# Expert tiles placed between the transforms of later batches, with the mixed rows scattered to their places by expert

## The chip, the cores and the metric

One core of a Trainium2 chip runs the kernel. The metric is device time in microseconds of one execution, median of several runs. The profiled execution is one run of its own, with its own time.

## What is computed

```python
X = np.fft.rfft(x, axis=1)                       # x: (8, 2496, 256)
y = np.fft.irfft(X * (filt_r + 1j * filt_i), n=2496, axis=1)
x = y.reshape(19968, 256)
expert_idx = token_ids * np.int64(2654435761) % np.int64(8)
for e in range(8):                               # w1: (8, 256, 1024), w2: (8, 1024, 256)
    mask = expert_idx == e
    out[mask] = np.maximum(x[mask] @ w1[e], 0.0) @ w2[e]
```

A filter in the frequency domain mixes the 2496 positions of each of 8 batches, channel by channel. Then each of the 19968 rows goes through the expert (two matrices with a ReLU between) that its token id names. All of it is in float32.

## The kernel before

**Transforms.** A batch's transform of length 2496 = 39 x 64 is done in three parts, each a row of matmuls, with a copy through DRAM between them. Part 1 (`stage1`, L161) has 8 units per batch: a load of `x`, two matmuls `pa` with the table `wf_t`, copies to `t1`, a store to the DRAM tile `d1`. Part 2 (`stage2`, L209) has 10 steps: `forward` makes `pb` from `d1` (tile `t2`, loaded four frequencies at a time by `load2`), VectorE multiplies it by the two filter tables, and one step later `back` makes `pc` with the table `e_t`; the result goes to the DRAM tile `d2`. Part 3 (`stage3`, L219) has 8 units: a load of `d2` (tile `t4`), two matmuls `pd` with `wi_t`, copies to `o`, and a store of 78 partitions to `xtok` in DRAM, where the rows stand in token order. Part 2 needs a whole `d1`, part 3 a whole `d2`. The loop at L372 runs part 2 of batch b, part 1 of b+1 and part 3 of b-1 beside each other, by a fraction of the step that each piece gets.

**Routing.** `route()` (L274) works out on VectorE from the token ids how many rows each expert has, and for each row a slot: rows of one expert lie together, padded to full tiles of 128. `slot_token` (156 indirect transfers on POOL) writes each row's number to its slot, and `idx_all` reads the list back. `chunk_i` holds for each of the NCH = 163 tiles its expert, and whether that differs from the expert two tiles before.

**Experts.** After the last transform the PSUM and SBUF pools are closed and opened anew. Per tile: `gather` (L425) fetches 128 rows of `xtok` by an indirect transfer, `turn` (L434) transposes them on TensorE, `up` (L442) does 16 matmuls with w1 into two PSUM tiles that ACT and VectorE clip at zero into `ht`, `down` (L458) does 8 matmuls with w2, VectorE copies the result, and POOL scatters it to `out`. Weights have two buffers that the tiles use in turn; `load_weights` (L343) loads a pair of 1 MB each on SP's queue, on the condition that the expert is another.

**Order.** All plain loads and stores are issued on SP's queue (constants on ACT's). In the transform stage a scheduler orders the engines' instructions; for the tiles SP's order is the program's.

## Time and profile before

| | |
|---|---|
| median of 3 runs | 1828.25 us (1825.52 to 1828.43) |
| the profiled execution | 1827.75 us |
| its span, first to last instruction | 1826.1 us |
| mean granted TensorE clock | 0.958 |
| TensorE busy | 1679.4 us (92%) |
| VectorE, ACT, POOL busy | 416.9, 248.8, 486.8 us |
| transfers | 208.91 MB, mean 114 GB/s |

The span is what the trace covers; the time has 1.65 us more around it. Busy time of TensorE is a union of overlapping matmuls whose ends are modelled, so a busy stretch is not one at its peak. PEclk is the granted clock as a part of the full one.

### The profile page before, as it was taken

How to read it: one execution, taken by the hardware profiler on the slowest of the kernel's cores; microseconds unless marked ns; L12 is line 12 of the kernel's file. 1: busy time of each engine (PE TensorE's matmuls, PEld its weight loads, DVE VectorE, ACT ScalarE, POOL GpSimd, SP SyncE). 2: the span in 40 equal slices, each digit the busy share in tenths (PEclk: the TensorE clock that was granted, in tenths of full speed). 3: DMA queues.
4: the chain of work that ended last, by engine and by line, in shares of the span. 5: the costliest groups of instructions: out<-in, count | busy, mean ns of one | idle time of the engine just before them, and what ended most of it. 6: DMA issues, size and time to landing. Idle time of an engine off the chain costs nothing.

```text
span 1826.1 us, 26491 instructions
## 1 busy us (share of the span) xinstructions
PE 1679.4 (92%) x9626; PEld 1393.6 (76%) x9626; DVE 416.9 (23%) x766; ACT 248.8 (14%) x416; POOL 486.8 (27%) x493
## 2 busy tenths in 40 slices
PE   4598579789798699999999999999999999999998
PEld 1365245445455299999999999999999999999997
DVE  2432123233232012112111211211211221121121
ACT  1122122222232100000000000000000000000000
POOL 0477760000000122222222222222222222222221
PEclk9999788898899599999999999999999999999999
DMA  9788887787786411131131131131131131122110
GB/s 214 187 226 238 212 245 218 207 254 223 206 257 180 137 36 35 57 111 36 38 126 39 38 126 38 36 129 39 35 130 36 39 129 36 39 83 81 39 36 8
DMA packets 111533, 208.91 MB, mean 114 GB/s; under 512 B 17546, under 2 KB 76556, under 8 KB 111085
## 3 DMA queue, kind: packets, MB, share of 16 engines
q1 hardware_dynamic: 88683, 158.47, 30.5%
q0 software_dynamic: 20640, 41.93, 7.4%
q10 hardware_dynamic: 2082, 6.82, 1.6%
q8 instruction: 78, 1.28, 0.3%
q14 instruction: 50, 0.41, 0.1%
HBM read 432.44 MB, written 83.92 MB: 283 GB/s over the span
## 4 chain that ended last, share of the span: by engine, by line
issue 47%; PE 24%; POOL 18%; DMA 8%; SPq 2%; POOLq 1%; DVE 1%; ACT 0%; ACTq 0%; DVEq 0%
POOL xg L429 9%; POOL out_dram L466 9%; PE pa L166 7%; PE pc L199 7%; PE pd L224 6%; DMA x<-in_x_dram 4%; PE pb L183 4%; DMA t<-d 3%; SPq L175 1%; SPq L206 0%; POOLq L466 0%; POOLq L429 0%; DMA d<-t 0%; ACT g L202 0%; DMA d<-g 0%
## 5 line engine op out<-in xcount | busy, mean ns | idle before, releaser
L450 PEld LDWEIGHTS ups<-xt,w 128*128 128x128 f32 x5216 | 610.0, 192 | 8.4
L450 PE MATMUL ups<-xt,w 128*128 128x128 f32 x5216 | 610.6, 275 | 0.0
L462 PE MATMUL dps<-w,ht 128*128 128x256 f32 x2608 | 589.9, 379 | 0.0
L462 PEld LDWEIGHTS dps<-w,ht 128*128 128x128 f32 x2608 | 482.8, 190 | 58.9
L429 POOL DMA_INDIRECT xg<-xtok,idx_all x163 | 167.1, 1025 | 733.3 <-DMA xtok<-o 366.5
L466 POOL DMA_INDIRECT out_dram<-osb,idx_all x163 | 166.2, 1019 | 488.9 <-DVE osb L465 488.9
L454 ACT ACTIVATE ht<-ups 128x512 f32<-128x512 f32 x163 | 97.3, 597 | 1089.1 <-PE ups L450 1089.1
L456 DVE TENSOR_SCALAR ht<-ups 128x512 f32<-128x512 f32 x163 | 112.7, 692 | 524.2 <-PE ups L450 524.2
L166 PE MATMUL pa<-x,wf_t 78*80 78x512 f32 x256 | 151.8, 731 | 82.4 <-DMA x<-in_x_dram 75.4
L335 POOL DMA_INDIRECT slot_tokens<-token,key_i x156 | 151.9, 973 | 110.7 <-DVE key_i L319 63.5
L465 DVE COPY osb<-dps 128x256 f32<-128x256 f32 x163 | 69.2, 425 | 423.2 <-PE dps L462 423.2
L166 PEld LDWEIGHTS pa<-x,wf_t 78*80 78x80 f32 x256 | 44.4, 179 | 157.7 <-issue 108.4
L224 PE MATMUL pd<-t,wi_t 80*78 80x512 f32 x256 | 135.6, 667 | 25.6 <-DMA t<-d 25.6
L199 PE MATMUL pc<-p,e_t 128*128 128x256 f32 x640 | 156.2, 388 | 0.0
L199 PEld LDWEIGHTS pc<-p,e_t 128*128 128x128 f32 x640 | 125.8, 197 | 22.5 <-issue 3.6
L188 DVE TENSOR_TENSOR p<-pb,filt 128x512 f32<-128x512 f32 x160 | 103.0, 686 | 147.9 <-PE pb L183 146.9
L183 PEld LDWEIGHTS pb<-t,d_t 128*128 128x128 f32 x320 | 65.5, 206 | 70.1 <-issue 53.8
L224 PEld LDWEIGHTS pd<-t,wi_t 80*78 80x78 f32 x256 | 41.1, 164 | 96.2 <-issue 81.2
L183 PE MATMUL pb<-t,d_t 128*128 128x256 f32 x320 | 90.4, 409 | 23.5 <-DMA t<-d 22.9
L202 ACT COPY g<-pc 128x512 f32<-128x512 f32 x80 | 46.9, 586 | 189.9 <-PE pc L199 181.9
L137 ACT COPY t<-pa 80x512 f32<-80x512 f32 x86 | 49.5, 582 | 152.9 <-PE pa L166 140.2
L437 PE MATMUL xps<-ident,xg 128*128 128x128 f32 x326 | 62.8, 275 | 7.9 <-DMA xg<-xtok,idx_all 7.9
(54 smaller groups left out, 247.5 us busy)
## 6 DMA issues: line engine op xcount, KB each, us to landing
w<-in_moe_w_dram SPq DMA_DIRECT2D x326, 1024.0 KB
d<-t SPq DMA_DIRECT2D x64, 320.0 KB
t<-d SPq DMA_DIRECT2D x80, 256.0 KB
d<-g SPq DMA_DIRECT2D x80, 256.0 KB
t<-d SPq DMA_DIRECT2D x64, 320.0 KB
x<-in_x_dram SPq DMA_DIRECT2D x64, 312.0 KB
xtok<-o SPq DMA_DIRECT2D x64, 312.0 KB
xg<-xtok,idx_all POOLq DMA_INDIRECT x163, 2.8
```

Source lines behind the costliest of these rows:

```text
L166: nc.tensor.matmul(out=ps[0:NK], lhsT=wf_t[:], rhs=xt[:, 2 * i:2 * i + 2, :], start=True, stop=True)
L183: nc.tensor.matmul(out=ps[:, i, :], lhsT=d_t[:, s, :], rhs=self.t2[s // SG][:, s % SG, :], start=True, stop=True)
L188: nc.vector.tensor_tensor(out=pt[:], in0=ps[:], in1=f_t[k][:, 2 * u:2 * u + 2, :], op=OP.mult)
L199: nc.tensor.matmul(out=ps[:, i, :], lhsT=e_t[:, k, 2 * u + i, :], rhs=pr[k][:, i, :], start=(k == 0), stop=(k == 1))
L224: nc.tensor.matmul(out=ps[0:NR], lhsT=wi_t[:], rhs=t4[:, 2 * i:2 * i + 2, :], start=True, stop=True)
L335: st = nc.gpsimd.indirect_dma_start(out=slot_dram[:, None], out_offset=bass.IndirectOffsetOnAxis(ap=key_i[:, j:j + 1], axis=0), in_=token[ ...
L429: nc.gpsimd.indirect_dma_start(out=xg[c][:, t, :], out_offset=None, in_=xtok[:], in_offset=bass.IndirectOffsetOnAxis(ap=idx_all[:, j:j + 1 ...
L450: nc.tensor.matmul(out=ps[:, i, :], lhsT=w1[:, dp, fp * P:(fp + 1) * P], rhs=xt[c][:, dp, :], start=(dp == 0), stop=(dp == DP - 1))
L454: nc.scalar.activation(out=dst, in_=ps[:], func=AF.Relu)
L456: nc.vector.tensor_scalar_max(dst, ps[:], 0.0)
L462: nc.tensor.matmul(out=ps[:], lhsT=ht[:, fp, :], rhs=w2[:, fp, :], start=(fp == 0), stop=(fp == FP - 1))
L466: st = nc.gpsimd.indirect_dma_start(out=out[:], out_offset=bass.IndirectOffsetOnAxis(ap=idx_all[:, c:c + 1], axis=0), in_=o[:], in_offset= ...
```

## The change

The rows' places are now made in stages. `stage_tiles` and the new part of `route` count, for the first 2, 4, 6 and all 8 batches, how many full tiles of 128 rows each expert has by then; the tiles that become full in a stage lie together in the DRAM tensor `xs`, by expert. So the first 30 tiles hold rows of batches 0 and 1 alone, the tiles up to 70 rows of the first 4 batches, those up to 108 of the first 6. Part 3 no longer stores to `xtok`: each unit makes 4 indirect scatters on POOL that put 78 rows each at their places in `xs`. A row is 272 words: 256 of data, and 16 that hold its number, which the scatter to `out` takes as its index. Places that stay empty in the last stage get 7 scatters of blank rows. A tile is then a plain load of 128 rows on SP's queue; the gathers and the `slot_token` transfers go.

The order is written out by hand for all engines. The list `pre` runs the parts 1 of batches 0 to 2, the parts 2 and 3 of batches 0 and 1, the routing, and the first two weight pairs. The list `main` gives every other transform piece a place among the tiles: a piece with key k runs in tile floor(k), between that tile's `turn` of the next tile and its `down`. Three batch steps lie in tiles 0 to 24, two more up to 62, the rest up to 100. Within a stage the tiles alternate between its lower and upper half. The two weight loads of a pair are issued apart, after `up` and after `down`. PSUM is shared: 4 buffers for the transforms, 2 for `up`, 1 each for `turn` and `down`. Copies of part 1 are all on ACT, those of part 3 all on VectorE; stores to `d1` and `d2` are issued on ACT's queue.

```diff
+STAGES = (2, 4, 6, 8)
+G = len(STAGES)
...
+def stage_tiles():
+    ends = [(S * b - E * (TB - 1)) // TB // 2 * 2 for b in STAGES[:-1]] + [NT]
+    out, first = [], 0
+    for end in ends:
+        half = (end - first + 1) // 2
+        out.append([first + i // 2 + (half if i % 2 else 0) for i in range(end - first)])
+        first = end
+    return out
...
+    xs = nc.dram_tensor("xs", (NT * TB, W), F32)
+    slot_dram = nc.dram_tensor("slots", (N,), I32)
...
+    ctx.enter_context(tc.manual_schedule())
...
+    fps = pool(ctx, "fps", 4, PSUM)
+    xps = pool(ctx, "xps", 1, PSUM)
+    ups = pool(ctx, "ups", 2, PSUM)
+    dps = pool(ctx, "dps", 1, PSUM)
...
-            nc.sync.dma_start(out=self.d1_rows[:, XG * u:XG * u + XG, :], in_=t1[:])
+                nc.scalar.copy(out=t1[:, 2 * i:2 * i + 2, :], in_=ps[0:NK])
+            nc.scalar.dma_start(out=self.d1_rows[:, XG * u:XG * u + XG, :], in_=t1[:])
...
-                    nc.sync.dma_start(out=self.d2[a0:a0 + SG, :, :].rearrange("s n c -> n s c"),
-                                      in_=self.g[64 * p:64 * p + 64, :, :])
+                    nc.scalar.dma_start(out=self.d2[a0:a0 + SG, :, :].rearrange("s n c -> n s c"),
+                                        in_=self.g[64 * p:64 * p + 64, :, :])
...
-            o = opool.tile([NR, XG, C], F32, name=f"o_{self.b}_{u}", tag="o")
+            o = opool.tile([NR, XG, W], F32, name=f"o_{self.b}_{u}", tag="o")
+            nc.gpsimd.iota(o[:, :, C:].bitcast(I32), pattern=[[1, XG], [0, W - C]],
+                           base=self.b * S + XG * u, channel_multiplier=N2 // 2)
             for i in range(XG // 2):
                 ps = fps.tile([P, 2, C], F32, name=f"pd_{self.b}_{u}_{i}", tag="f")
                 nc.tensor.matmul(out=ps[0:NR], lhsT=wi_t[:], rhs=t4[:, 2 * i:2 * i + 2, :],
                                  start=True, stop=True)
-                evac(o[:, 2 * i:2 * i + 2, :], ps[0:NR])
-            st = nc.sync.dma_start(out=self.rows(xtok.ap(), u), in_=o[:])
-            tc.declare_no_dep(st.ins, group="xtok_rows", reason="distinct rows")
-            tc.add_to_no_dep_group("xtok_rows", st.ins)
-    batches = [Batch(0)]
-    for u in range(2):
+                nc.vector.tensor_copy(out=o[:, 2 * i:2 * i + 2, 0:C], in_=ps[0:NR])
+            for i in range(XG):
+                j = XG * u + i
+                scatter(o[:, i, :], sidx[:, self.b, j:j + 1], f"xs_{self.b}")
+    def scatter(rows, index, group):
+        st = nc.gpsimd.indirect_dma_start(
+            out=xs[:], out_offset=bass.IndirectOffsetOnAxis(ap=index, axis=0),
+            in_=rows, in_offset=None, bounds_check=NT * TB - 1, oob_is_err=False)
+        for other in ["xs_pad", "xs_read"] + [f"xs_{b}" for b in range(B)]:
+            tc.declare_no_dep(st.ins, group=other, reason="distinct rows")
+        tc.add_to_no_dep_group(group, st.ins)
...
+    def weights(i, which):
+        if i >= NT:
+            return
+        if i < 2:
+            if which == 0:
+                ws[i] = [wpool.tile([P, DP, F], F32, name=f"w1_{i}"), wpool.tile([P, FP, C], F32, name=f"w2_{i}")]
+        elif which == 0:
+            ws[i] = ws[i - 2]
+        e = nc.sync.value_load(chunk_i[0:1, 0, i:i + 1], min_val=0, max_val=E - 1)
+        kw = {}
+        if i >= 2:
+            kw = {"cond": nc.sync.value_load(chunk_i[0:1, 1, i:i + 1], min_val=0, max_val=1)}
+        if which == 0:
+            nc.sync.dma_start(out=ws[i][0][:], in_=moe_w1[bass.ds(e, 1)].rearrange("one (dp p) f -> p (one dp) f", p=P), **kw)
+        else:
+            nc.sync.dma_start(out=ws[i][1][:], in_=moe_w2[bass.ds(e, 1)].rearrange("one (fp p) d -> p (one fp) d", p=P), **kw)
...
+        nc.vector.tensor_tensor(acc[:], run[:], over(off[:, 0, :], NJ), op=OP.add)
+        for g in range(1, G):
+            nc.vector.tensor_tensor(tmp[:], run[:], over(full_t[:, g, :], NJ), op=OP.is_ge)
+            nc.vector.tensor_tensor(tmp[:], tmp[:], over(step[:, g, :], NJ), op=OP.mult)
+            nc.vector.tensor_tensor(acc[:], acc[:], tmp[:], op=OP.add)
+        nc.vector.tensor_mul(acc[:], acc[:], mask[:])
...
+        nc.gpsimd.dma_start(out=slot_dram[:].rearrange("(p j) -> p j", p=P), in_=slot_i[:])
+        nc.gpsimd.dma_start(out=sidx[:], in_=slot_dram[:].rearrange("(b p n) -> p b n", b=B, p=NR))
...
+        for q in range(NQP):
+            scatter(blank[:], at_i[:, q:q + 1], "xs_pad")
...
+        ps = fps.tile([P, 2, C], F32, name="ce_ps", tag="f")
+        for q in range(2):
+            nc.tensor.matmul(out=ps[0:1, 0, q * P:(q + 1) * P], lhsT=seg[:, q:q + 1], rhs=ident[:],
+                             start=True, stop=True)
...
+    def part1(b, t0, t1):
+        bt = batches[b]
+        at = [t0 + (t1 - t0) * u / NU for u in range(NU)]
+        step = (t1 - t0) / NU
+        out_ = [(at[u], lambda u=u: bt.stage1(u)) for u in range(NU)]
+        out_ += [(at[u] - 1.9 * step, lambda u=u: bt.load1(u)) for u in range(3 if b == 0 else 0, NU)]
+        return out_
...
+        out_ += [(max(at[2 * g] - 4.5 * step, ready), lambda g=g: bt.load2(g)) for g in range(NS // SG)]
...
+    pre = part1(0, -100, -81) + [(-80.9, route), (-80.8, dup_filters)]
+    pre += part1(1, -79, -60) + part2(0, -75, -50, -80)
+    pre += part2(1, -45, -25, -59) + part3(0, -44, -25)
+    pre += part3(1, -20, -1) + part1(2, -19, -2)
+    pre += [(-30 + i, lambda i=i: (weights(i, 0), weights(i, 1))) for i in range(2)]
+    pre.sort(key=lambda t: t[0])
+    bounds = [0.0, 9.0, 18.0, 25.0, 44.0, 63.0, 84.0, 101.0]
+    main, ready = [], 0.0
+    for k, b in enumerate(range(3, B + 2)):
+        t0, t1 = bounds[k], bounds[k + 1]
+        d = t1 - t0
+        if b - 1 < B:
+            main += part2(b - 1, t0 + 0.01 * d, t0 + 0.9 * d, ready)
+        if b < B:
+            main += part1(b, t0 + 0.02 * d, t0 + 0.62 * d)
+            ready = t0 + 0.65 * d
+        if b - 2 >= 2:
+            main += part3(b - 2, t0 + 0.3 * d, t1)
+    main.sort(key=lambda t: t[0])
+    for _, piece in pre:
+        piece()
+    rctx.close()
...
+    def load(i):
+        q = tiles[i]
+        xg[i] = gath.tile([P, W], F32, name=f"xg_{i}", tag="xg")
+        ld = nc.sync.dma_start(out=xg[i][:], in_=xs[q * TB:(q + 1) * TB, :])
+        for b in range(STAGES[stage_of[i]], B):
+            tc.declare_no_dep(ld.ins, group=f"xs_{b}", reason="the tiles of a stage hold tokens of its batches alone")
+        tc.add_to_no_dep_group("xs_read", ld.ins)
...
-            out=out[:], out_offset=bass.IndirectOffsetOnAxis(ap=idx_all[:, c:c + 1], axis=0),
+            out=out[:], out_offset=bass.IndirectOffsetOnAxis(ap=xg[i][:, C:C + 1].bitcast(I32), axis=0),
...
-    ctx.enter_context(tc.manual_schedule(engines={mybir.EngineType.SP}))
-    for c in range(min(3, NCH)):
-        gather(c)
+        del xg[i]
+    for i in range(4):
+        load(i)
     turn(0)
-    for c in range(NCH):
-        ht = work.tile([P, FP, CH], F32, name=f"ht_{c}", tag="ht")
-        if c + 3 < NCH:
-            gather(c + 3)
-        up(c, ht)
-        if c + 1 < NCH:
-            turn(c + 1)
-        down(c, ht)
-        if c + 2 < NCH:
-            load_weights(c + 2)
+    for i in range(NT):
+        ht = work.tile([P, FP, TB], F32, name=f"ht_{i}", tag="ht")
+        if i + 4 < NT:
+            load(i + 4)
+        up(i, ht)
+        weights(i + 2, 0)
+        if i + 1 < NT:
+            turn(i + 1)
+        while main and main[0][0] < i + 1:
+            main.pop(0)[1]()
+        down(i, ht)
+        weights(i + 2, 1)
+    assert not main
```

TensorE at an expert tile before (`ups` are the up matmuls, `xps` the transposes of the next tile, `dps` the down matmuls):

```order
L450 MATMUL ups_0_9642<-xt_9601,w_1_1001 128x128 x8
L450 MATMUL ups_1_9652<-xt_9601,w_1_1001 128x128 x8
L437 MATMUL xps_9662<-ident,xg_9510 128x128 x2
L462 MATMUL dps_9667<-w_1_1002,ht_9637 128x256 x8
L450 MATMUL ups_0_9706<-xt_9665,w_0_988 128x128 x8
```

Up runs into the transposes, and these into down, with nothing between. TensorE at the second tile now (`pa`, `pb`, `pc` are the transforms' matmuls):

```order
L534 MATMUL ups_1_1404<-xt_1300,w_1_911 128x128 x8
L523 MATMUL xps_1433<-ident,xg_1246 128x128 x2
L185 MATMUL pa_2_0_1442<-x_2_1331,wf_t 80x512
L185 MATMUL pa_2_1_1445<-x_2_1331,wf_t 80x512
L202 MATMUL pb_2_1449<-t_2_1_1309,d_t 128x256 x2
L221 MATMUL pc_1_1456<-p_1_0_1336,e_t 128x256
L221 MATMUL pc_1_1456<-p_1_1_1338,e_t 128x256
...
L546 MATMUL dps_1466<-w_1_912,ht_1391 128x256 x8
```

A unit of part 1 of batch 3 and a step of part 2 of batch 2 now stand between the transposes and the down matmuls of this tile.

TensorE behind the first batch's part 1, before (`cnt_ps` are the count matmuls of the routing):

```order
L166 MATMUL pa_7_1_212<-x_7_190,wf_t 80x512
L293 MATMUL cnt_ps<-cnt,ones 128x8
L294 MATMUL cnt_ps<-cnt,before 128x8
L183 MATMUL pb_0_276<-t_0_0_265,d_t 128x256 x2
L166 MATMUL pa_0_0_293<-x_0_286,wf_t 80x512
```

Part 2 of batch 0 followed the two count matmuls. TensorE at the same place now:

```order
L185 MATMUL pa_7_1_218<-x_7_202,wf_t 80x512
L349 MATMUL cnt_ps<-cntg,ones 128x32
L351 MATMUL cnt_ps<-cnt,before 128x8
L436 MATMUL ce_ps<-ident,seg 1x128 x2
L185 MATMUL pa_0_0_364<-x_0_212,wf_t 80x512
L185 MATMUL pa_0_1_367<-x_0_212,wf_t 80x512
```

Two matmuls `ce_ps`, which take the routing's result `seg` from VectorE, now stand ahead of all matmuls of batch 1 and of part 2.

SP's queue at the first tile now (`w` are weights, `xg` a tile's rows, `t_2_0` to `t_2_2` the first loads of part 2 of batch 2):

```order
L283 DMA w_0_869<-in_moe_w_dram 128x2x1024
L175 DMA x_0_1302<-in_x_dram 78x1024
L175 DMA x_1_1304<-in_x_dram 78x1024
L194 DMA t_2_0_1306<-d_2_1005 64x4x256 x2
L194 DMA t_2_1_1309<-d_2_1005 64x4x256 x2
L194 DMA t_2_2_1312<-d_2_1005 64x4x256 x2
L175 DMA x_2_1331<-in_x_dram 78x1024
L175 DMA x_3_1356<-in_x_dram 78x1024
...
L285 DMA w_0_870<-in_moe_w_dram 128x8x256
L515 DMA xg_1392<-xs 128x272
```

Transform loads now stand between the two weight loads of a tile, on the same queue.

## Rows read from the trace of the kernel before

**Rows 1.** The page's slices: 40 equal parts of the span.

```profile
PE   4598579789798699999999999999999999999998
...
PEclk9999788898899599999999999999999999999999
...
GB/s 214 187 226 238 212 245 218 207 254 223 206 257 180 137 36 35 57 111 36 38 126 39 38 126 38 36 129 39 35 130 36 39 129 36 39 83 81 39 36 8
```

**Rows 2.** Windows: stretch, length, busy time by engine, PEclk, DMA share, GB/s.

```profile
599.50:627.20 27.70, 27.56 (x32) 8.02 (x32) 3.43 (x5) 5.83 (x11) 0.00 (x0) 0.50 0.53 150
636.10:1818.70 1182.60, 1182.60 (x8148) 1114.97 (x8146) 235.08 (x487) 97.32 (x163) 328.60 (x322) 1.00 0.19 61
1818.70:1826.10 7.40, 0.04 (x1) 0.00 (x0) 0.42 (x1) 0.00 (x0) 0.97 (x1) 0.67 0.00 0
```

**Rows 3.** Timeline of TensorE, 585 to 660 us: start, duration, operation, idle before.

```profile
599.55 27.56 PE L224 MATMUL pd<-t,wi_t 80*78 80x512 f32 x32 [8.69 <-DMA t<-d]
...
636.11 5.70 PE L450 MATMUL ups<-xt,w 128*128 128x128 f32 x32
...
645.10 3.73 PE L450 MATMUL ups<-xt,w 128*128 128x128 f32 x32
...
648.89 3.62 PE L462 MATMUL dps<-w,ht 128*128 128x256 f32 x16
652.35 3.73 PE L450 MATMUL ups<-xt,w 128*128 128x128 f32 x32
```

**Rows 4.** Timeline of TensorE in the transform stage, at full clock.

```profile
156.61 1.88 PE L166 MATMUL pa<-x,wf_t 78*80 78x512 f32 x4
158.33 1.03 PE L183 MATMUL pb<-t,d_t 128*128 128x256 f32 x4
159.19 1.89 PE L199 MATMUL pc<-p,e_t 128*128 128x256 f32 x8
160.92 1.88 PE L224 MATMUL pd<-t,wi_t 80*78 80x512 f32 x4
162.64 1.03 PE L183 MATMUL pb<-t,d_t 128*128 128x256 f32 x4
```

**Rows 5.** Timeline of TensorE: count matmuls, and the first pb of batches 0 and 1.

```profile
52.87 0.43 PE L293 MATMUL cnt_ps<-cnt,ones 128*128 128x8 f32 x2
...
73.43 2.05 PE L183 MATMUL pb<-t,d_t 128*128 128x256 f32 x4 [19.70 <-DMA t<-d]
...
118.25 1.03 PE L183 MATMUL pb<-t,d_t 128*128 128x256 f32 x4
```

**Rows 6.** Timeline of VectorE in the routing.

```profile
54.17 0.17 DVE L300 CAST chunks<-chunks_i 128x8 f32<-128x8 int32 x1
54.38 0.17 DVE L302 TENSOR_TENSOR_SCAN upto<-ones,chunks 128x8 f32<-128x8 f32 x1
...
58.45 1.44 DVE L308 TENSOR_TENSOR run<-run,base 128x1248 f32<-128x1248 f32 x1
...
62.03 2.35 DVE L311 TENSOR_REDUCE slot<-run 128x156 f32<-128x1248 f32 x1
```

**Rows 7.** Groups of instructions: busy us and mean ns of one, idle before.

```profile
L359 DVE COPY filt<-filt 64x5120 f32<-64x5120 f32 x1 | 2.8, 2822 | 15.6 <-DMA filt<-in_filt_r_dram 15.6
```

**Rows 8.** Timeline of POOL: indirect transfers of 4-byte rows, one behind the other.

```profile
67.34 0.97 POOL L335 DMA_INDIRECT slot_tokens<-token,key_i  x1 [0.31 <-issue]
```

**Rows 9.** The tile xg: its gathers of 128 rows of 1 KB, ns min/median/max.

```profile
L429 POOL DMA_INDIRECT xg<-xtok,idx_all x163: 999/1025/1049, 631.5 to 1779.5; - x163
...
DMA to landing us min/median/max: 2.8/2.8/6.1
```

**Rows 10.** Waits of SP: for whom, us in total, times, longest.

```profile
SPq L356 <- PE dps L462: 521.9, 161, 3.3
```

**Rows 11.** The chain that ended last: start, us, what (a load of x).

```profile
268.40 6.25 DMA x<-in_x_dram
```

**Rows 12.** Windows in which the second expert's weights arrive, columns as in rows 2.

```profile
780.00:784.00 4.00, 4.00 (x26) 3.66 (x25) 0.79 (x3) 0.00 (x0) 1.10 (x2) 1.00 0.98 370
```

More of the change, by code (lines that the diff above doesn't have):

```diff
@@ L33 @@
 NU = N2 // 2 // XG
-CH = 128
-TB = CH // P
-NCH = (N + E * (CH - 1)) // CH
-NCOL = NCH * TB
+TB = 128
+NT = (N + E * (TB - 1)) // TB
+W = C + 16
 NJ = N // P
@@ new lines, in route @@
+        nc.vector.memset(full[:, 0, :], 0.0)
+        nc.vector.tensor_copy(full[:, 1:, :], full_i[:])
+        made = rpool.tile([P, G, E], F32)
+        nc.vector.tensor_sub(made[:], full[:, 1:, :], full[:, 0:G, :])
+        last = rpool.tile([P, G * E], F32)
+        nc.vector.tensor_tensor_scan(last[:], ones[:, 0:G * E], made[:].rearrange("p g e -> p (g e)"), 0.0,
+                                     op0=OP.mult, op1=OP.add)
+        first = rpool.tile([P, G, E], F32)
+        nc.vector.tensor_sub(first[:].rearrange("p g e -> p (g e)"), last[:],
+                             made[:].rearrange("p g e -> p (g e)"))
@@ new lines, in route @@
+        off = rpool.tile([P, G, E], F32)
+        nc.vector.tensor_sub(off[:], first[:], full[:, 0:G, :])
+        nc.vector.tensor_scalar(off[:], off[:], float(TB), None, op0=OP.mult)
+        step = rpool.tile([P, G, E], F32)
+        nc.vector.tensor_sub(step[:, 1:, :], off[:, 1:, :], off[:, 0:G - 1, :])
+        full_t = rpool.tile([P, G + 1, E], F32)
+        nc.vector.tensor_scalar(full_t[:], full[:], float(TB), None, op0=OP.mult)
+        base = rpool.tile([P, E], F32)
+        nc.vector.tensor_sub(base[:], ps[:, 1, 0:E], ends[:, 0:E])
@@ L412, with part2 @@
-    assert not slots
-    nc.sync.dma_start(out=idx_all[:], in_=slot_dram[:].rearrange("(p c) -> p c", p=P))
-    fctx.close()
-    gath = pool(ctx, "gath", 4)
+    def part1(b, t0, t1):
[5 more added lines that the diff above has]
+        return out_
+    def part2(b, t0, t1, ready):
+        bt = batches[b]
+        n = NS // 2 + 1
+        at = [t0 + (t1 - t0) * u / n for u in range(n)]
+        step = (t1 - t0) / n
+        out_ = [(at[u], lambda u=u: bt.stage2(u)) for u in range(n)]
+        out_ += [(max(at[2 * g] - 4.5 * step, ready), lambda g=g: bt.load2(g)) for g in range(NS // SG)]
+        return out_
@@ new lines, in part3 @@
+    def part3(b, t0, t1):
+        bt = batches[b]
+        at = [t0 + (t1 - t0) * u / NU for u in range(NU)]
+        step = (t1 - t0) / NU
+        out_ = [(at[u], lambda u=u: bt.stage3(u)) for u in range(NU)]
+        out_ += [(at[u] - 1.9 * step, lambda u=u: bt.load4(u)) for u in range(NU)]
+        return out_
+    order = stage_tiles()
+    tiles = sum(order, [])
+    stage_of = [g for g, o in enumerate(order) for _ in o]
+    pre = part1(0, -100, -81) + [(-80.9, route), (-80.8, dup_filters)]
```

287 lines of the change are left out of this document (116 added, 171 removed).

## The prediction

> **What bounds the kernel now.** I read the slices of the page first [rows 1]. There the reader should see two stages with different limits. In the first 14 slices of 45.65 us TensorE's share goes up and down between 4 and 9 tenths, while the transfers stay near 200 to 250 GB/s: that is the transform stage, paced by transfers and by handovers through DRAM. From slice 15 on TensorE is at 9 and the transfers fall to some 40 GB/s: the expert stage, paced by TensorE alone. The windows say it exactly [rows 2]: from 636.10 to 1818.70 TensorE is busy for all of 1182.60 us, so 163 tiles cost 7.255 us each, and 7.40 us follow the last matmul. In the timeline a tile is up, down and the next up, without a gap [rows 3]. So the time is a sum of three: the first up matmul at 636.11, then 1182.6, then 7.4, which is the span of 1826.1 us. The change can win only in the first term, and it has to pay in the second.
>
> The profiled execution took 1827.75 us, 1.65 more than its span and 0.5 below the median of 1828.25. My sum is made against that execution.
>
> **The sum.** New span = F + 1182.6 + T + S + 7.4. F is the new start of the first up matmul, T the transform matmuls that now stand between tiles, S the waits of TensorE behind that start. Against the old span this is a gain of 636.1 - F - T - S.
>
> **T, transform matmuls between tiles.** The rows at full clock give a unit of part 1 as 1.72 us, pb 0.86, pc 1.73 and a unit of part 3 as 1.72 (start to start) [rows 4]. A batch has 8 units of part 1 (13.8 us), 10 of part 2 (25.9) and 8 of part 3 (13.8). Left for the tiles are 5 batches of part 1, and 6 of part 2 and of part 3: 69 + 155.4 + 82.8 = 307.2 us. They cost the same wherever they stand, as long as the clock is at its full level, and the expert stage has it at 1.00 throughout [rows 2].
>
> **F, the start.** Four steps follow one another: part 1 of batch 0 with the routing; part 1 of 1 with part 2 of 0; part 2 of 1 with part 3 of 0; part 3 of 1 with part 1 of 2.
> - *Batch 0.* The count matmuls start at 52.87 [rows 5]. Constants, loads and stores are the same megabytes, all copies are now ACT's, and ACT has two small transfers less to issue and one more; I keep 53.
> - *Routing.* Before, nothing on TensorE waited for it. Now the two `ce_ps` matmuls stand in TensorE's order ahead of batch 1, and wait for VectorE's chain. It has 12 passes of 128x1248 (1.44 us, about 1.47 with the step to the next), one reduction (2.35) and some 43 small ones at 0.21 from start to start [rows 6]: 17.6 + 2.4 + 9.0 = 29 us. TensorE goes on at 82. The filter copy (2.82 us [rows 7]) and five small operations follow on VectorE, 4 us in which TensorE runs two units of part 1 (3.4).
> - *Second step.* The same work took from 73.43 to 118.25 before [rows 5]: 44.8 us. It ends at 82 + 4 - 3.4 + 44.8 = 127.
> - *Third step.* Part 3 needs batch 0's whole DRAM copy: the old handover kept TensorE idle for 8.69 us [rows 3]. Then 25.9 + 13.8 = 39.7 us of matmuls. The scatters are new: 4 per unit on POOL, each with 78 rows of 1088 bytes. Nothing like it is in the trace; the nearest are POOL's indirect transfers, 0.97 us plus 0.31 to the next for 4-byte rows [rows 8], 1.02 to 1.05 for 1 KB rows [rows 9]. I take 1.28, between 0.78 (by the count of rows, 78 of 128) and 1.36 (1.05 + 0.31): 32 of them are 41 us, beside the matmuls. TensorE is done at 127 + 8.7 + 39.7 = 175.
> - *Fourth step.* Another handover, 8.7, to 184. Then only pa and pd run. [...] So 8 x 6.9 = 55 us, to 239, and POOL's 41 us lie beside it. [...]
> - *Last scatters to first up.* Copy 0.7, four scatters 5.1, landing 2.8 [rows 9], load of a tile and turn some 4: 13. Before it was 9.0, from the end of the last pd at 627.11 to 636.11 [rows 3]. F = 252, with ends at 238 (clock released) and 275 (scatters and handovers at their upper ends, the third step paced by its 10.5 MB and 4.2 MB of weights at 207 GB/s, 71 us in place of 48 [rows 1]).
>
> **S, waits between the tiles.** SP meets the expert stage in order: each tile's second weight load waits for that tile's down matmuls, so a transform's load goes out when TensorE reaches its tile. SP has the room: it idles 521.9 us for those waits now [rows 10]; the two further value loads per tile and the loads fit there. But the lead is short. By the table 118 load steps lie among the tiles: 3 in the tile that uses them, 27 one tile ahead, the rest two or more. A load took 6.25 us at transform traffic [rows 11]; one tile with its pieces is 10 to 13 us, so it is hidden.
> - The three without lead are in tile 0: 1.15 MB at 230 GB/s and the delay of a transfer, 8 us, and after it a stretch at half clock, some 4 (the first up after a pause took 5.70 for 3.73 [rows 3]).
> - Tiles 0 to 24 carry three transform steps: 181 us of tiles and 146 of transforms, with 61 MB to move (x, two DRAM copies each way, tiles, six weight pairs). At 207 GB/s, the lowest of slices 3 to 12 [rows 1], that is 296 us, under 327. So transfers do not set it on average; for bunched pieces in tiles 18 to 24 I take 10, with ends at 0 and 40.
> - Weights: these token ids give 39 loads of a pair (2.1 MB) where there were 16, 25 of them among the transforms. Four megabytes went at up to 370 GB/s beside tiles with TensorE fully busy [rows 12]: nothing, while two tiles of lead cover it; the bound is below.
> - The tile loads are plain rows in place of gathers, stores go out on ACT rather than on SP; both lie beside TensorE's work and are counted at nothing. Their cover is that work; without it they are part of the cases below. PSUM buffers are halved (two for up, one for down and for turn); copies of 0.4 to 0.7 us lie under 3.6 us matmul groups.
> S = 22.
>
> **Sum:** 252 + 1182.6 + 307.2 + 22 + 7.4 = 1771 us of span, 1773 us of time, 3.0% below.
>
> **Rivals.**
> - *Loads queue behind weights (slower).* SP's queue is one line. A pair of 2.1 MB put ahead of a load adds some 8 us at the rate of [rows 12] to its 6.25, 14 in all, over the 10 to 13 of a one-tile lead. The step gained is 636.1 - 252 - 307.2 = 77; 12 go to tile 0. If each of the 25 pairs holds TensorE for more than 65 / 25 = 2.6 us, the change loses. At 4 us each the time is 1773 - 10 + 100 = 1863. For it: 27 loads with one tile of lead, and bunched pairs around tiles 29 to 31. Against it: pairs spaced four tiles apart early, and the old stage took its pairs without a gap. 0.12.
> - *Scatters land one after another (slower).* Then a unit of part 3 costs 4 x 2.8 = 11.2 us, a batch 90, and the third and fourth steps grow by 42 and 35: 1850. Against it: POOL issued indirect transfers every 1.28 us [rows 8] while one took 2.8 to land [rows 9], so several were under way. [...] The trace here has no 78-row scatter. 0.04.
> - *The clock rises in the fourth step.* 14 us less: 1759. 0.15.
> - *It does not overlap*, because a stage's loads wait for later scatters: excluded, since those scatters need loads that stand behind in SP's order, and the program would never end.
> - *Gain used up*: F and S both near their upper ends, S about 55: within 0.2%. 0.04.
>
> **How the numbers follow.** My case gets 0.65. What a measurement of this kernel tells from no change is about 0.2%, 3.7 us; its runs lie 2.9 us apart. Faster: 0.65 + 0.15 = 0.80; same 0.04; slower 0.12 + 0.04 = 0.16. The range goes from F at 238 and S near 7 (1744) to F and S both late, short of the slower rivals: 1825.
>
> **What would show it.** The first up near 252, with TensorE idle for about 29 us behind the count matmuls and a clock of 0.50 in the stretch of pa and pd before it. Between the first up and the last down 1182.6 + 307 + about 22 us, with the waits in tile 0 and around tiles 18 to 24. Steady tiles of 7.25 us behind tile 100. It is wrong if TensorE's idle time between tiles passes 77 us, if it waits for `x` or `t` in most transform tiles, if w loads end its waits, or if the start lies beyond 300.

## The result, and the profile after

The changed kernel takes **1773.49 us** (median of 4 runs, 1772.01 to 1775.07) against 1827.88 of the kernel before: a ratio of **0.9705, 95% interval 0.9688 to 0.9722**. It is faster by 3%, and the forecast was 1773. The profiled execution has a span of 1770.3 us and took 1772.01.

The slices of the page for the changed kernel:

```profile
PE   3398778999999999999999999999999999999998
...
PEclk9998659999999999999999999999999999999999
...
GB/s 218 101 205 210 261 125 152 160 162 225 184 195 217 175 264 182 128 121 194 123 196 98 160 197 125 123 108 125 187 52 228 62 111 68 104 78 89 83 81 12
```

Beside [rows 1] the first stage has shrunk from 14 slices to 6. From slice 8 on TensorE is at 9 up to the last slice, and the transfers that filled the old first stage are spread over the rest: 98 to 264 GB/s in slices 7 to 24, where the old expert stage had some 40 in most slices. The windows cut this at the steps of the forecast (stretch, length, busy time of TensorE, weight loads, VectorE, ACT, POOL, then clock, DMA share, GB/s):

```profile
0.00:58.70 58.70, 28.21 (x32) 7.88 (x33) 5.41 (x9) 9.56 (x16) 1.53 (x11) 1.00 0.86 208
58.70:89.30 30.60, 0.92 (x6) 0.84 (x5) 27.88 (x56) 5.04 (x2) 2.05 (x3) 1.00 0.26 62
89.30:135.00 45.70, 45.46 (x156) 29.43 (x157) 16.86 (x26) 14.17 (x25) 9.38 (x8) 1.00 0.76 211
143.60:186.30 42.70, 42.69 (x148) 28.23 (x148) 20.76 (x32) 5.26 (x9) 26.41 (x33) 0.92 0.90 254
197.60:252.40 54.80, 54.80 (x64) 16.20 (x64) 10.30 (x15) 9.30 (x16) 27.88 (x36) 0.50 0.62 173
285.50:1762.90 1477.40, 1476.87 (x9163) 1295.97 (x9161) 375.30 (x698) 175.50 (x298) 349.98 (x402) 1.00 0.47 141
```

The second line is the routing: VectorE works, TensorE has 0.92 us of matmuls in 30.6, and the transfers fall to 62 GB/s. The fifth is pa and pd alone, at a clock of 0.50. The 1.00 in the first line is not the speed of its matmuls: the 16 matmuls of pa from 44.98 take 13.94 us (timeline below), some 3.43 for a unit, as at 0.50 in the fifth window (3.41) and not as at full clock (1.72 [rows 4]). The last is the main reading: from the first down matmul to the last, TensorE is idle for 0.53 of 1477.40 us at full clock. In the timeline of TensorE (start, duration, operation, idle before) the waits all lie ahead of that:

```profile
44.98 13.94 PE L185 MATMUL pa<-x,wf_t 78*80 78x512 f32 x16 [15.95 <-ACT t L187]
58.71 0.47 PE L349 MATMUL cnt_ps<-cntg,ones 128*128 128x32 f32 x2
...
89.26 1.01 PE L436 MATMUL ce_ps<-ident,seg 128*1 128x128 f32 x4 [29.68 <-DVE seg L433]
...
143.55 3.67 PE L249 MATMUL pd<-t,wi_t 80*78 80x512 f32 x4 [7.49 <-DMA t<-d]
...
197.55 3.67 PE L249 MATMUL pd<-t,wi_t 80*78 80x512 f32 x4 [11.27 <-DMA t<-d]
...
260.86 0.66 PE L523 MATMUL xps<-ident,xg 128*128 128x128 f32 x2 [8.44 <-DMA xg<-xs]
262.04 6.08 PE L534 MATMUL ups<-xt,w 128*128 128x128 f32 x32 [0.52 <-DVE xt L525]
...
276.75 2.05 PE L202 MATMUL pb<-t,d_t 128*128 128x256 f32 x4 [8.41 <-DMA t<-d]
...
285.54 3.62 PE L546 MATMUL dps<-w,ht 128*128 128x256 f32 x16
...
1747.93 3.73 PE L534 MATMUL ups<-xt,w 128*128 128x128 f32 x32
...
1755.18 3.73 PE L534 MATMUL ups<-xt,w 128*128 128x128 f32 x32
```

The first up comes at 262.04 in place of 636.11 [rows 3]. A tile behind the transforms still takes 1755.18 - 1747.93 = 7.25 us.

### The profile page after: what moved, and what is told of

It reads as the page before. It is cut to its first block, busy times and chain, and to the rows that moved or that the text cites. A ratio compares the mean times of both kernels' runs of the same rounds, so it can differ in the third digit from the quotient of the medians.

```text
span 1770.3 us, 27290 instructions
## 1 busy us (share of the span) xinstructions
PE 1665.8 (94%) x9630; PEld 1390.9 (79%) x9630; DVE 463.8 (26%) x848; ACT 222.9 (13%) x373; POOL 427.2 (24%) x503
## 4 chain that ended last, share of the span: by engine, by line
PE 70%; issue 20%; DMA 5%; POOL 3%; DVE 2%; POOLq 0%; ACT 0%; SPq 0%; ACTq 0%; DVEq 0%
PE ups L534 22%; PE dps L546 21%; PE pc L221 8%; PE pa L185 7%; PE pd L249 7%; PE pb L202 4%; POOL out_dram L550 3%; DMA d<-t 2%; PE xps L523 1%; DMA x<-in_x_dram 1%; DMA t<-d 1%; DMA d<-g 1%; DMA w<-in_moe_w_dram 0%; DVE acc L391 0%; DVE tmp L390 0%
## 5 line engine op out<-in xcount | busy, mean ns | idle before, releaser
L546 PEld LDWEIGHTS dps<-w,ht 128*128 128x128 f32 x2608 | 488.5, 190 | 80.3 <-issue 19.2
L550 POOL DMA_INDIRECT out_dram<-osb,xg x163 | 159.9, 981 | 904.7 <-DVE osb L549 878.2
L257 POOL DMA_INDIRECT xs<-o,sidx x256 | 240.9, 941 | 344.4 <-issue 197.6
L221 PE MATMUL pc<-p,e_t 128*128 128x256 f32 x640 | 152.2, 381 | 0.2 <-ACT g L224 0.2
L221 PEld LDWEIGHTS pc<-p,e_t 128*128 128x128 f32 x640 | 121.8, 191 | 18.1 <-ACT g L224 0.6
L251 DVE COPY o<-pd 78x512 f32<-78x512 f32 x128 | 87.6, 686 | 114.0 <-PE pd L249 69.6
L187 ACT COPY t<-pa 80x512 f32<-80x512 f32 x128 | 73.2, 581 | 224.4 <-PE pa L185 199.0
L202 PEld LDWEIGHTS pb<-t,d_t 128*128 128x128 f32 x320 | 60.8, 195 | 42.9 <-issue 30.8
L202 PE MATMUL pb<-t,d_t 128*128 128x256 f32 x320 | 85.0, 389 | 8.4 <-DMA t<-d 8.4
L224 ACT COPY g<-pc 128x512 f32<-128x512 f32 x80 | 46.8, 585 | 268.4 <-PE pc L221 235.7
```

Of the source, the lines that this page charges most:

```text
L202: nc.tensor.matmul(out=ps[:, i, :], lhsT=d_t[:, s, :], rhs=self.t2[s // SG][:, s % SG, :], start=True, stop=True)
L221: nc.tensor.matmul(out=ps[:, i, :], lhsT=e_t[:, k, 2 * u + i, :], rhs=pr[k][:, i, :], start=(k == 0), stop=(k == 1))
L251: nc.vector.tensor_copy(out=o[:, 2 * i:2 * i + 2, 0:C], in_=ps[0:NR])
L257: st = nc.gpsimd.indirect_dma_start(out=xs[:], out_offset=bass.IndirectOffsetOnAxis(ap=index, axis=0), in_=rows, in_offset=None, bounds_ch ...
L546: nc.tensor.matmul(out=ps[:], lhsT=ht[:, fp, :], rhs=w2[:, fp, :], start=(fp == 0), stop=(fp == FP - 1))
L550: st = nc.gpsimd.indirect_dma_start(out=out[:], out_offset=bass.IndirectOffsetOnAxis(ap=xg[i][:, C:C + 1].bitcast(I32), axis=0), in_=o[:], ...
```

## The experiments

Theory: the gain is the overlap. Transfers that paced the first stage lie under tile matmuls, where their lead hides them, and only the start F is left to pay. Rivals: the gain comes from the other edits (plain loads, order by hand); loads queue behind weights; the start is paced by transfers, whatever TensorE waits for.

The kernels ran on several chips. Beside the first four experiments (block, routing, clock, loads ahead) the kernel before took 2004.64 us (1999.85 to 2010.84), beside all others 1829 to 1831 (medians). The changed kernel itself was never timed on that chip, and what slows the old one there is not known, so the ratios of those four (0.9368, 0.8799, 0.8886 and 0.8876) are not compared with the others; they are read by their traces and compared with one another. Their own offset is small: the block kernel, which has the change's program up to the first up, has it at 267.19 where the control below has 261.40, and from the first down to the last the other three are some 6 us longer. An estimate for the change there is 1785 us: the 1763.86 of the routing kernel and the 21.4 by which its first up comes sooner than the block's.

**The change and the kernel before, again.** No edit.

> The changed kernel unaltered, on the chip of the other runs of this call, since the kernel before took 2005 us there in the runs beside the first four experiments, and 1828 us where the change was first timed. Theory (that chip moves data a little slower, and only the kernel before meets it in the expert stage): the time is 1775 to 1780 us, with the first up near 267 as in the run with the block in tile 0, whose program is the same up to there. Rival (the whole chip is slower): some 1940 us.

> The kernel before unaltered, to see in its trace where 2005 us come from in place of 1828. Theory A: the transform stage is the same and each of the 163 tiles takes 8.3 us in place of 7.26, because TensorE waits for gathers or for VectorE's copies. Theory B: the first stage, which is paced by transfers, takes 810 us in place of 636 at some 170 GB/s, and the tiles are the same.

The changed kernel took 1776.29 us (1771.52 to 1776.75), ratio 0.9708 (0.9683 to 0.9733): the same gain. But these two ran on a chip where the kernel before is at 1830.56 (1836.35 in its own single run), so neither expectation on the slow chip was put to the test. Why the kernel before needs 2005 us there stays open; no trace of it from that chip exists. This run is the control below; its window from the first down to the last is that of the change:

```profile
285.00:1762.40 1477.40, 1476.87 (x9163) 1295.96 (x9161) 374.92 (x698) 175.64 (x298) 350.34 (x402) 1.00 0.47 141
```

**All transform pieces in tile 0**, without overlap:

```diff
-    bounds = [0.0, 9.0, 18.0, 25.0, 44.0, 63.0, 84.0, 101.0]
+    bounds = [t / 102.0 for t in (0.0, 9.0, 18.0, 25.0, 44.0, 63.0, 84.0, 101.0)]
```

> The rest of the change stays (plain tile loads, scatters by expert, order by hand), but all transform pieces of batches 2 to 7 that lay among tiles 0 to 100 now stand in tile 0, ahead of its down matmuls. Theory (the gain is the overlap alone: transform matmuls that fill no gap any more cost what their transfers take): the first up stays near 262 us, the block in tile 0 takes 370 to 410 us, by its 85 MB or so of loads and stores at the 207 to 230 GB/s of the start (307 us of matmuls lie in it), and the time is 1840 to 1880 us, at or above the kernel before. Rival (the gain comes from the dropped gathers, the scatters in place of a row-order store, and the hand-written order): the time stays within 10 us of 1773.

1876.45 us (1872.65 to 1882.03), 100 above the control, and above the 1830 that the kernel before takes elsewhere. The timeline and a window over the block:

```profile
282.17 2.05 PE L202 MATMUL pb<-t,d_t 128*128 128x256 f32 x4 [9.26 <-DMA t<-d]
...
668.81 4.24 PE L546 MATMUL dps<-w,ht 128*128 128x256 f32 x16
```

```profile
282.20:668.80 386.60, 346.74 (x1072) 201.77 (x1073) 138.95 (x212) 80.05 (x140) 178.02 (x224) 0.89 0.79 225
```

The pieces take 668.8 - 282.2 = 387 us where their matmuls are worth 307, at 225 GB/s and a clock of 0.89: of the 80 us more, TensorE is idle for 40, and the other 40 are matmuls that run below the full clock. This is read from one execution, whatever the chip. So the overlap is the gain, and beside the kernel before as it runs elsewhere the other edits together do not bring it. Of the 100 us some 10 may be the chip's, by the offset above. On this chip itself the block kernel is faster than the kernel before (0.9368); since no trace shows what slows that one, this tells nothing of the edits.

**Tiles in sequence**, 27 more weight pairs:

```diff
-        out.append([first + i // 2 + (half if i % 2 else 0) for i in range(end - first)])
+        out.append(list(range(first, end)))
```

> The tiles of a stage follow one another in the order of their places in place of alternating between the two halves of the stage, so two tiles on end have the same expert and both weight buffers are loaded within two tiles: 66 loads of a pair in place of 39, 27 more. Theory (loads of the transforms are hidden by one or two tiles of lead, and a pair of 2.1 MB ahead of them costs no more than it takes, which the lead covers except where two pairs stand together): waits among the tiles stay under 20 us and the time is 1773 to 1793. Rival (each pair holds the transform loads behind it by some 4 us): 27 x 4 = 108 us more, 1880.

1775.13 us (1771.08 to 1778.51), against 1776.29 of the control. From the first down to the last:

```profile
292.00:1769.40 1477.40, 1476.86 (x9163) 1295.96 (x9161) 374.90 (x698) 175.64 (x298) 350.19 (x402) 1.00 0.58 179
```

The window is 1477.40 us again, with 179 GB/s in place of 141 and not one more wait. The rival of loads behind weights falls: 4 us per pair would have been 108.

**The counting early.** `route` is cut ahead of `past`: counts, slots and the blank rows' scatters run after the second unit of part 1 of batch 0, and only the table of experts (`past` to `chunk_i`) stays behind the eighth:

```diff
+        return last
+    def route_experts():
+        last = counted[0]
...
-    pre = part1(0, -100, -81) + [(-80.9, route), (-80.8, dup_filters)]
+    pre = part1(0, -100, -81) + [(-97.0, lambda: counted.append(route())), (-80.9, route_experts), (-80.8, dup_filters)]
```

> The counting part of the routing is emitted after the second unit of part 1 of batch 0 instead of after the eighth, so that VectorE's chain runs beside the remaining six units, and the two ce_ps matmuls stand where they did. Theory (TensorE's 29.7 us wait for VectorE's chain lies on the path that sets the start): the wait at ce_ps falls under 5 us, the first up comes at 262 - 25 to 30 = 232 to 237 us, and the time is 1743 to 1750 us. Rival (the start is paced by transfers, and the pause at ce_ps only lets loads and stores catch up: 62 GB/s were moved in it): the wait reappears as waits for x, t or copies in the next step, and the time stays within 6 us of 1773.

1763.86 us (1762.11 to 1764.88). TensorE's timeline:

```profile
59.38 1.01 PE L441 MATMUL ce_ps<-ident,seg 128*1 128x128 f32 x4
...
74.05 3.67 PE L185 MATMUL pa<-x,wf_t 78*80 78x512 f32 x4 [2.93 <-DMA x<-in_x_dram]
...
245.82 5.40 PE L540 MATMUL ups<-xt,w 128*128 128x128 f32 x32 [0.52 <-DVE xt L531]
```

The wait at `ce_ps` is gone, and the first up comes at 245.82. On the same chip the block kernel, which has the change's program up to there, had it at 267.19: 21.4 us sooner, of 29.7. The rest came back in the second step: 4.6 us as waits for x and t, as the rival said, and some 4 as matmuls behind them that ran longer than in the change (a group of pc 3.21 us in place of 1.89). The rival has only this rest. The size was missed: I expected 232 to 237 and 1743 to 1750.

**Batch 0's stores on SP's queue.**

```diff
-            nc.scalar.dma_start(out=self.d1_rows
+            (nc.sync if self.b == 0 else nc.scalar).dma_start(out=self.d1_rows
```

> The d1 stores of batch 0 alone go out on SP's queue in place of ACT's, where 6.6 MB of constants stand ahead of them. Theory (the count matmuls came 6 us later than forecast because ACT's third copy waited 20.6 us for a d1 store that stood behind the constants): the 16 us wait of pa for ACT falls under 5, the count matmuls start at 40 to 50 us in place of 58.7, and the first up comes 8 to 15 us earlier: 1760 to 1766. Rival (the first 58 us are paced by the 12 MB that they move at 208 GB/s, in whatever order): x or t waits take the place of that wait, and the time is 1770 to 1776.

1772.33 us (1769.52 to 1775.13), ratio 0.9701 (0.9675 to 0.9728): no difference to the control that can be told. TensorE's timeline, the window up to the count matmuls, and from the same stretch a line of ACT's timeline and a line of SP's waits (us in total, times, longest):

```profile
29.97 3.67 PE L185 MATMUL pa<-x,wf_t 78*80 78x512 f32 x4 [6.91 <-DMA x<-in_x_dram]
39.65 7.09 PE L185 MATMUL pa<-x,wf_t 78*80 78x512 f32 x8 [6.00 <-DMA x<-in_x_dram]
...
55.36 0.47 PE L349 MATMUL cnt_ps<-cntg,ones 128*128 128x32 f32 x2
...
273.16 2.04 PE L202 MATMUL pb<-t,d_t 128*128 128x256 f32 x4 [9.02 <-DMA t<-d]
...
285.03 3.62 PE L546 MATMUL dps<-w,ht 128*128 128x256 f32 x16
```

```profile
0.00:55.40 55.40, 28.75 (x33) 7.41 (x34) 5.40 (x9) 9.51 (x16) 1.53 (x11) 1.00 0.80 212
```

```profile
31.47 1.06 ACT L187 COPY t<-pa 80x512 f32<-80x512 f32 x2 [13.07 <-DMA d<-t]
```

```profile
SPq L188 <- ACT t L187: 31.8, 7, 9.9
```

TensorE's 16 us wait for ACT is gone, but waits for x took its place (26.6 us in all), and the count matmuls start 3 us sooner. The stretch moves 212 GB/s in place of 208. The rival has the outcome; that these 58 us are paced by their bytes is not shown. The edit made another wait: SP issues in the program's order, and the x loads now stand behind the stores, where SP waits 31.8 us for ACT's copies, while ACT's third copy still waits 13.07 us for a store to land. And the first up does come 3.6 us sooner than in the control (257.83 and 261.40); the first down does not (285.03 and 285.04), since the matmuls behind the wait for t in tile 0 take 11.9 us in place of 8.8, where the starts of [rows 4] make 6.9: a clock of 0.58 in place of 0.79.

**Tile 0's loads**, ahead of all tile loads, and then behind the first of them:

```diff
+    while main[0][0] <= 0.0:
+        pre.append(main.pop(0))
```

> The five loads that the transform pieces of tile 0 need (two of x, three of t) are issued ahead of the first tile loads and weights' rest instead of in tile 0. Theory (the 8.4 us wait for t between the first up and the first down is the missing lead of those loads): that wait goes and the time is 1763 to 1766. Rival (the loads only take the place of the tile loads, so that the first up comes later by what is saved): the time stays within 3 us of 1773.

```diff
     for i in range(4):
         load(i)
+        while i == 0 and main[0][0] <= 0.0:
+            main.pop(0)[1]()
```

> The five loads for the transform pieces of tile 0 are issued behind the first tile load and ahead of the next three, so that they neither wait for the first up (as in the change) nor stand ahead of the first tile load (as in the run that put them before all tile loads). Theory: the first up stays within 2 us of 262, the 8.4 us wait for t goes, 1766 to 1769. Rival (the transfer after batch 2's last d1 store decides, wherever the load stands): no difference.

The first took 1778.38 us (1777.37 to 1782.52). Its timeline:

```profile
271.19 0.66 PE L525 MATMUL xps<-ident,xg 128*128 128x128 f32 x2 [12.75 <-DMA xg<-xs]
...
284.52 3.62 PE L548 MATMUL dps<-w,ht 128*128 128x256 f32 x16
```

The wait for t is gone, but the wait for `xg` ahead of the first up is 12.7 us in place of 8.5, and the first up comes at 272.37, 5.2 us later than the block kernel's on that chip. The rival has that; it does not have the balance. The first down follows the first up by 12.2 us in place of 23.5, so it comes at 284.52, where the change on that chip would have it at some 291 (267.19 and 23.5 to 24, an estimate). By that some 6 us are won, and by the estimate of 1785 us for the change there some 7. The second took 1769.08 (1767.86 to 1772.42), ratio 0.9688 (0.9663 to 0.9713). Its timeline:

```profile
260.69 6.54 PE L534 MATMUL ups<-xt,w 128*128 128x128 f32 x32 [0.52 <-DVE xt L525]
272.43 0.66 PE L523 MATMUL xps<-ident,xg 128*128 128x128 f32 x2 [5.20 <-DMA xg<-xs]
...
281.63 3.62 PE L546 MATMUL dps<-w,ht 128*128 128x256 f32 x16
```

The first up stays, the wait for t is gone, and tile 1's rows are late in its stead: 5.2 us. The first down comes 281.63 - 260.69 = 20.9 us after the first up, where the change needs 285.54 - 262.04 = 23.5. So 2.6 of 8.4 us are won here, less than I expected, and too little for the ratios to tell apart.

**Clock: other matmuls in the fourth step.** Per unit of part 3 of batch 1:

```diff
+            if self.b == 1:
+                spare = fps.tile([P, 2, C], F32, name=f"spare_{u}", tag="f")
+                for i in range(2):
+                    for k in range(2):
+                        nc.tensor.matmul(out=spare[:, i, :], lhsT=e_t[:, k, 2 * u + i, :],
+                                         rhs=f_t[k][:, 2 * u + i, :], start=(k == 0), stop=(k == 1))
```

> Four more matmuls of 128 rows by 128 columns by 256 stand in each of the 8 units of part 3 of batch 1, in the fourth step; they go to a PSUM buffer that nothing reads. Theory A (the granted clock follows what kind of matmul runs: full-width ones mixed in lift it): the fourth step shows 1.00 in place of 0.50, pa and pd take 28 us and the new ones 14, so 42 in place of 55 (POOL's 40 us of scatters lie beside it), and the time is 1760. Rival B (the clock stays at the lower level after a pause whatever runs): the new matmuls add 8 x 3.45 = 27.6 us at that level and the time is 1800.

1781.43 us (1780.00 to 1783.19), where an estimate for the change on that chip is 1785. Three windows: from the first pd to the end of the last, around the first pa and the first added group, and behind it; then lines of TensorE's timeline:

```profile
203.50:253.30 49.80, 48.25 (x120) 23.37 (x120) 10.20 (x15) 9.30 (x16) 27.34 (x34) 0.83 0.66 189
206.00:213.50 7.50, 7.50 (x14) 3.88 (x13) 0.95 (x2) 1.16 (x2) 3.98 (x5) 0.51 0.90 231
213.50:230.00 16.50, 16.50 (x53) 8.48 (x52) 4.11 (x6) 3.49 (x6) 10.36 (x13) 1.00 0.60 188
```

```profile
206.98 3.62 PE L185 MATMUL pa<-x,wf_t 78*80 78x512 f32 x4
...
213.57 1.88 PE L255 MATMUL pd<-t,wi_t 80*78 80x512 f32 x4
...
233.28 4.93 PE L185 MATMUL pa<-x,wf_t 78*80 78x512 f32 x6 [1.47 <-PE pa L185]
```

The clock does rise, to 1.00 behind the first added group, and a group of pa or pd falls from 3.42 to 1.72 us start to start. It does not last: a wait of 1.5 us is followed by matmuls at the lower speed again (the six of pa from 233.28 take 4.7 us up to the next group, 2.6 at full clock), the mean is 0.83, and the step takes 49.8 us in place of 54.8, with the added matmuls in it. Theory A has the rise of the clock, not the time: the first up comes 3.4 us sooner than the block kernel's on that chip (263.78 and 267.19), not 13, and the whole is some 4 us under the estimate.

**Clock: pa in the handover.**

```diff
-    pre += part3(1, -20, -1) + part1(2, -19, -2)
+    pre += part3(1, -20, -1) + part1(2, -27, -8)
```

> The eight units of part 1 of batch 2 start 8 key steps earlier, so that three or four of them stand ahead of the first pd of batch 1 and TensorE has matmuls in the handover from the third to the fourth step (11.3 us idle, then a granted clock of 0.50 for 54.8 us). Theory A (the clock falls because TensorE has nothing to do in that handover, and pa and pd alone then don't raise it again): the clock stays at 1.00, pa and pd take 28 us, POOL's scatters (32 at 1.25 = 40 us) set the rest of the step, and the first up comes 20 to 28 us earlier: 1745 to 1755 us on the first chip. Rival B (pa and pd are held at 0.50 whatever was before): only the idle time goes, 8 to 11 us, first up at 252 to 256 us, and the time is 1763.

1772.50 us (1768.40 to 1773.97), ratio 0.9679 (0.9651 to 0.9707), inside the control's. TensorE's timeline:

```profile
197.76 3.67 PE L185 MATMUL pa<-x,wf_t 78*80 78x512 f32 x4 [4.80 <-DMA x<-in_x_dram]
203.71 3.67 PE L249 MATMUL pd<-t,wi_t 80*78 80x512 f32 x4 [2.28 <-DMA t<-d]
```

The handover was not filled: x came late behind the same transfers, the first pd, which waits for the load of d2, starts 6 us later than in the change (203.71 in place of 197.55), and the clock is 0.50 again. The first up is where it was, at 261.51. This tells nothing between theory A and rival B, since TensorE did pause.

**Three edits together**: the counting early, batch 0's stores on SP, tile 0's loads behind the first tile load.

> Three edits in one: the counting part of the routing early, batch 0's d1 stores on SP's queue, tile 0's transform loads behind the first tile load. Theory (they lie one behind the other on the path to the first tiles, so their gains add): 16 to 21 of the routing, 8 to 12 of the stores and 8 of tile 0, first up at 225 to 235 us, 1735 to 1745. Rival (with the routing out of the way the second step is paced by transfers): only the routing's 16 and tile 0's 8 are left, 1750 to 1754.

**1743.29 us** (1741.80 to 1744.25), ratio 0.9541 (0.9518 to 0.9565). The first up, and the window from the first down to the last:

```profile
235.66 6.03 PE L540 MATMUL ups<-xt,w 128*128 128x128 f32 x32 [0.52 <-DVE xt L531]
```

```profile
255.90:1733.40 1477.50, 1476.86 (x9163) 1295.95 (x9161) 375.21 (x698) 175.50 (x298) 350.00 (x402) 1.00 0.47 141
```

The time is inside the theory's 1735 to 1745, and the gains do add, but two of the three terms are not the expected ones, so the total is partly luck. Against the control the first up is 25.7 us sooner and tile 0 3.4 shorter, together the 29.1 between the spans (1769.8 and 1740.7); the window behind is the same 1477.5. On this chip the store edit alone has the first up at 257.83, so the routing brings 22.2 of the 25.7 (expected 16 to 21) and the stores 3.6 (8 to 12); tile 0 brings 3.4 (8).

**Part 2 of batch 2 in the fourth step**, on top of these three:

```diff
-    pre += part2(1, -45, -25, -59) + part3(0, -44, -25)
-    pre += part3(1, -20, -1) + part1(2, -19, -2)
-    pre += [(-30 + i, lambda i=i: (weights(i, 0), weights(i, 1))) for i in range(2)]
+    pre += part2(1, -45, -25, -59) + part3(0, -44, -25) + part1(2, -46, -27)
+    pre += part3(1, -20, -1) + part2(2, -20.5, -2, -26)
+    pre += [(-12 + i, lambda i=i: (weights(i, 0), weights(i, 1))) for i in range(2)]
...
-        if b - 1 < B:
+        if 3 < b <= B:
```

> On top of the three edits together (1743 us): part 1 of batch 2 goes beside the third step, part 2 of batch 2 beside part 3 of batch 1 in the fourth step and so out of the tiles, and the first two weight pairs are loaded in the middle of the fourth step in place of the handover ahead of it. Theory (the clock of the fourth step is at the lower level because only the narrow matmuls pa and pd run there; pb and pc, which fill all 128 rows and columns, lift it as the added matmuls did): the third step grows by 5.1 MB at some 254 GB/s, 20 us, the fourth shrinks from 55 to about 41 us at a clock of 1.00 (POOL's 40 us of scatters beside it), and 25.9 us of matmuls leave the tiles: 1743 + 20 - 14 - 26 = 1723. Rival (the clock stays at 0.50 behind the handover): the fourth step takes 79 us, 24 more, and the time is 1743 + 20 + 24 - 26 = 1761.

**1721.91 us** (1720.41 to 1723.69), ratio 0.9397 (0.9378 to 0.9416), the best of all. Windows of the third step, the fourth step, and from the first down to the last:

```profile
120.30:175.80 55.50, 55.50 (x176) 32.59 (x176) 22.49 (x34) 13.32 (x23) 28.65 (x36) 0.92 0.85 226
186.20:237.20 51.00, 44.61 (x148) 28.34 (x148) 21.54 (x33) 5.86 (x10) 27.70 (x35) 0.89 0.82 239
257.30:1712.30 1455.00, 1454.40 (x9059) 1276.27 (x9057) 364.63 (x682) 170.62 (x290) 350.15 (x402) 1.00 0.47 141
```

The sum came out, its terms only in part, so that it came out is partly luck. The third step grew by 13 us (55.5 for 42.7), not 20. The fourth has the clock at 0.89 in place of 0.50, and pd with the 25.9 us of pb and pc takes 51.0 us where pd with pa took 54.8; I expected 41, and a 5.7 us wait for t is among the rest. The first up is 12.1 us later than with the three edits (247.79 and 235.66), but tile 0, which no longer holds part 2 of batch 2, has its first down 9.5 us behind it in place of 20.3; this term the sum did not have. So the first down is only 1.4 us later (257.3 and 255.9), and the tiles behind it lost 1477.5 - 1455.0 = 22.5 us. The rival falls: the clock did not stay at 0.50. What the weights' new place adds was not tried apart.

## Why the prediction was right

**The structure held.** Span = F + 1182.6 + T + S + 7.4, with T = 307.2: the tiles' window is 1477.4 us at full clock with 0.53 us idle, in the change, in the control and with 27 pairs more. With the first up at 262.04, S is 1770.3 - 262.04 - 1182.6 - 307.2 - 7.4 = 11 us.

**F was 252 and is 262, too small by 10.** Step by step:

| step | forecast | measured |
|---|---|---|
| count matmuls start | 53 | 58.71 |
| routing, until TensorE goes on | 29 | 30.6 |
| second step, with what precedes it | 45.4 | 46.8 |
| handover | 8.7 | 7.5 |
| third step | 39.7 | 42.7 |
| handover | 8.7 | 11.3 |
| fourth step | 55 | 54.9 |
| last matmul to first up | 13 | 9.6 |

The largest miss is the first. "Constants, loads and stores are the same megabytes" is true, and what I made of it was not: ACT's third copy waited 20.6 us for the store of the first, which stood on ACT's queue behind the constants. Moving these stores to SP's queue gave back 3 us of 5.7; the waits for x that came in their place have more than one possible cause (the run above), so the other 2.7 stay open. One thing more lies in this step: the last four units of pa take 13.7 us up to the count matmuls, twice what they take at full clock (4 x 1.72 = 6.9), and nothing was tried on that. ACT's timeline of the change shows the wait:

```profile
22.73 1.06 ACT L187 COPY t<-pa 80x512 f32<-80x512 f32 x2 [0.39 <-ACT t L187]
23.83 0.31 ACTq L188 DMA_DIRECT2D d<-t  x1
44.34 1.06 ACT L187 COPY t<-pa 80x512 f32<-80x512 f32 x2 [20.55 <-DMA d<-t]
```

In the third step, the first matmuls behind the handover ran at the lower clock (3.46 us from the first pd at 143.55 to the next group, 1.72 at full clock; 0.92 in the window), which I had not counted there. The second handover is longer than the one of [rows 3]: 264 GB/s were being moved in it, with two weight pairs among them, but I have not separated these. With the weights moved out of it, in the last experiment, TensorE idles 9.2 us there (waits for t of 2.6 and 6.6); other loads were moved there too.

**S was 22 and is 11, too large by 11.** The load wait in tile 0 was right: 8 forecast, 8.4 measured. So was the cost of the lower clock, 4 forecast and 4.3 measured (2.4 in the first up, 1.9 behind the wait for t, at 0.79), as far as it goes: some 1.7 of it stand in the 1182.6 already, for the old first tile took 645.10 - 636.11 = 8.99 us [rows 3]. The term that failed is the bunched transfers in tiles 18 to 24: 10 us forecast, and they cost nothing, by the window above. (The lowest of slices 3 to 12, from which that term was weighed, is 206 GB/s and not 207 [rows 1]; the 296 us come out of it all the same.) So F and S were wrong by the same amount in opposite directions, and 1773 is better than its terms.

**The clock of the fourth step** was taken from the row at 0.50 [rows 2], and that row held. The 55 us are 16 units at 3.45, as 8 units of pd took 27.56 us there [rows 3], with pa counted like pd; measured are 54.80 us busy at 0.50. The rival 14 us faster (0.15) is those 55 less POOL's 41, with the clock up. It falls, and the lower end of F, 238, with it: no run shows this step at 41 us (49.8 and 51.0 with other matmuls in it). With pa and pd alone the clock was 0.50 in the change, in the control and with the three edits together, TensorE busy for 54.80 of 54.80 us, and with pa in the handover, busy for 44.34 of 45.00. It rose in the same step when e_t matmuls stood between them, in two kernels: to 1.00 behind the first added group, and to 0.89 over the step with pb and pc.

**The scatters** were costed at 1.28 us and take 0.94 + 0.30:

```profile
L257 POOL DMA_INDIRECT xs<-o,sidx x256: 927/938/962, 147.1 to 1307.2; - x128
...
DMA to landing us min/median/max: 2.4/3.2/8.2
```

A landing takes 3.2 us in the median while one is issued every 1.24, so several are under way, and the rival that they land one by one falls. Its price was added up wrong: a batch of 90 us of scatters against the 39.7 of the third step is 50 more, not 42, so 1858 us. **Loads behind weights** falls by the run with 66 pairs. **No overlap** was excluded by argument; the block kernel shows what it would have cost: 387 us for 307 of matmuls, and some 90 to 100 us of time.

**What is still open**: the slow chip for the kernel before alone, 2.7 us of the first step and whether bytes or the order of the queues pace it, and why the handover of the third to the fourth step is longer than the other.

## What to carry to other kernels

When one stage is paced by transfers and handovers and the next by TensorE alone, put the first among the second: ask only which piece of the first must come ahead, and price that chain step by step, since nothing else is left in the time. Behind it, loads with one tile of lead were hidden even with 27 more weight pairs on their queue, so the next gains lie in the start: a chain on another engine that TensorE waits for (22 of 29.7 us came back by running it earlier), then a step whose matmuls leave the clock low (0.50 here; useful work of another kind moved there put the first down only 1.4 us later and took 22.5 us out of the tiles). A store moved to another queue can take its wait along: loads behind it then wait in its place (26.6 us of waits for x here).
